# Converting the weights of an attention-and-SoLU kernel two pieces at a time, with a longer search for the order

## The chip, the cores and the metric

The kernel runs on one core of one Trainium2 chip. The time is what the device takes for one execution, in microseconds (us), as a median over runs. A core has engines that run side by side, each through its own instructions in a fixed order: PE multiplies matrices (PEld is its loading of the stationary operand), DVE works on vectors, ACT does activations, scalings and copies, POOL does elementwise work and masks, and SP issues most of the transfers from memory (DMA). An engine waits for another only through semaphores.

## The reference

Attention within a narrow window plus attention to summaries of blocks, then a feed-forward layer whose activation is `h * softmax(h)`, normalised:

```python
k_sum = k.reshape(B, H, nb, block, D).max(axis=3)      # block = 32
v_sum = v.reshape(B, H, nb, block, D).mean(axis=3)
scores = concat([where(|i-j| < 16, scale * q @ k.T, -1e9),
                 scale * q @ k_sum.T + log(32)])
x = softmax(scores) @ concat([v, v_sum])               # 4 x 8 heads x 768 x 64
h = x @ w_in                                           # 3072 x 512 @ 512 x 1024
solu = h * softmax(h)
ln = (solu - mean) / sqrt(var + 1e-6) * g_ln
out = ln @ w_out                                       # 1024 x 512
```

`w_in`, `w_out` and `g_ln` arrive as they are; `w_in` and `w_out` reach the kernel as 64-bit words (the weights are doubles), everything else as 32-bit floats.

## The kernel before

**Tiling.** The 3072 rows are 24 tiles `t` of 128 rows. For each tile two pairs of heads are scored (`scores`, PE tile `s`), exponentiated on ACT, turned (`values_turn`, tile `t`) and multiplied with the values (`values`, tile `x`). The result is split into a high and a low part, `xh` and `xl`, so that three matmuls give one product of nearly full precision. `first(t)` multiplies them with `w_in` into two halves `h` of 512 columns (24 matmuls, L697), takes the maximum, the exponential, the product and the mean (`he`), and gets the reciprocal deviation; `turn(t)` transposes `he` into `lh` and `ll`; `second(t)` multiplies these with `w_out` into `o` (24 matmuls, L775), scales and stores it. `second` runs four tiles behind `first` (LAG).

**Weights.** Each weight matrix is loaded in eight pieces of 128 rows by 512 doubles (`load_w`, L356, on the SP queue), that is 128 x 1024 words. A piece of `w_in` is a row block `c` and a half `nh` of the columns; a piece of `w_out` is a row block `f`. `rounded` (L359) makes a float of each double: the high words are converted on ACT or DVE (L368, L370), the low words likewise (L374, L376), the sign is combined in (L379, DVE), the high part is shifted (L383, DVE) and the two are added (`tt`, L288 on DVE or L289 on POOL). Then `split_w_in` copies the rounded part (`copy`, ACT or DVE) and subtracts it (L288 or L289), and `split_w_out` does the same with the row's `g_ln` as a factor (L400 on ACT, L402 on DVE). The scratch `st` of a piece of `w_in` lies in the five buffers of `he`, that of `w_out` in the two buffers of `vrow`. The result `hl` takes the place of the raw words.

**Order.** The code first collects operations: an engine or several that could do it, a planned cost on each, and what it depends on. `Plan.issue` then simulates the engines with these costs (`order`): at each step the operation that can begin first goes next, ties and some exceptions by a due time `due`, which comes from the operations that need the result; that of an SP load is its place in the program, at the start the string LOADS (`w` a piece of `w_in`, `k` keys, `q` queries, `r` rows of `v` for the means, `v` the first values, `Q` and `V` the next ones). It makes 64 such plans, each with other random noise on all due times, the SP loads' too, and takes the one in which PE ends first. The instructions are issued in that order, and every engine keeps to it. Where the plan has PE idle before 80 us, matmuls of zeros are put in (`keep_up`, L900).

## Time and profile before

| | us |
|---|---|
| median of 3 runs | 397.38 (397.09 to 397.52) |
| profiled execution, its time | 397.45 |
| its span, first to last instruction | 395.7 |
| PE busy | 386.6 (98%) |
| DVE busy | 275.4 (70%) |
| ACT busy | 248.7 (63%) |
| POOL busy | 97.9 (25%) |

The page divides the span in 40 slices of 9.9 us; each digit is the busy share of a slice in tenths:

```profile
PE   8999998999999999999999999999999999999996
DVE  4999998999789866577767657657657654554330
ACT  3889686999798756658558466468466463533411
POOL 4224010416837221236220121221021021101100
DMA  7999992136277320463330410430310000000011
```

PE's row counts matmuls of zeros as busy. DVE and ACT are near full in the first ten slices and at some two thirds or less behind them; the transfers fill the first six. Weights are converted only in those first ten slices.

### The profile page before, as it was taken

Reading aid. Unit: us, or ns where it says so; the run is one execution under the profiler, and the core shown is the slowest. Engines: PE = TensorE matmul, PEld = TensorE weight load, DVE = VectorE, ACT = ScalarE, POOL = GpSimd, SP = SyncE. Lnnn points to the kernel's source line nnn. Section 1 sums busy time; section 2 is a strip of 40 time slices with the busy share of each in tenths; the row PEclk is TensorE's granted clock in tenths of the full one; section 3 lists DMA queues with packets and bytes.
Section 4 is the critical chain, followed back from the end, with each engine's and each line's share of the span. In section 5 each row is a group of like instructions: output and inputs, shape, how many; then the busy total and the mean of one; then the engine's idle time right before and its main releaser. Section 6 shows DMA issues by size and latency. Waiting matters only on the chain.

```text
span 395.7 us, 9677 instructions
## 1 busy us (share of the span) xinstructions
PE 386.6 (98%) x3697; PEld 298.3 (75%) x3703; DVE 275.4 (70%) x884; ACT 248.7 (63%) x746; POOL 97.9 (25%) x245
## 2 busy tenths in 40 slices
PE   8999998999999999999999999999999999999996
PEld 3436766677878888878888888878888887878776
DVE  4999998999789866577767657657657654554330
ACT  3889686999798756658558466468466463533411
POOL 4224010416837221236220121221021021101100
PEclk9999999999999999999999999999999999999999
DMA  7999992136277320463330410430310000000011
GB/s 287 411 410 369 409 329 78 56 113 185 70 248 208 113 103 0 141 175 104 123 112 2 150 66 27 156 73 28 108 48 27 2 28 27 16 12 28 27 55 53
DMA packets 14994, 49.24 MB, mean 124 GB/s; under 512 B 1836, under 2 KB 2092, under 8 KB 13412
## 3 DMA queue, kind: packets, MB, share of 16 engines
q1 hardware_dynamic: 11084, 41.89, 30.8%
q10 hardware_dynamic: 3864, 6.74, 4.7%
q8 instruction: 29, 0.48, 0.5%
q14 instruction: 17, 0.14, 0.1%
HBM read 40.11 MB, written 6.29 MB: 117 GB/s over the span
## 4 chain that ended last, share of the span: by engine, by line
PE 85%; DMA 6%; ACT 3%; DVE 2%; issue 1%; ACTq 1%; SPq 1%; DVEq 0%
PE o L775 35%; PE h L697 30%; PE x L672 6%; PE s L578 5%; PE t L633 3%; PE lt L633 3%; DMA st_v<-in_vr 3%; DMA raw<-in_w_in 2%; DMA vt<-vsum 2%; PE vs_ps L459 1%; PE x L900 1%; ACT he L712 1%; DVE he L720 1%; ACT at L281 1%; PE x L664 1%
## 5 line engine op out<-in xcount | busy, mean ns | idle before, releaser
L775 PE MATMUL o<-w,lh 128*128 128x512 f32 (+1 forms) x400 | 128.0, 390 | 0.1
L697 PE MATMUL h<-w,xh 128*128 128x512 f32 x384 | 127.0, 398 | 0.4 <-DVE he L720 0.4
L605 ACT ACTIVATE e<-e,nm 128x120 f32<-128x120 f32 x192 | 73.1, 385 | 25.0 <-DVE nm L597 25.0
L775 PEld LDWEIGHTS o<-w,lh 128*128 128x128 f32 x400 | 74.1, 188 | 18.5 <-issue 2.4
L697 PEld LDWEIGHTS h<-w,xh 128*128 128x128 f32 x384 | 72.1, 188 | 18.9 <-ACT e L605 0.8
L775 PE MATMUL o<-w,ll 128*128 128x512 f32 (+1 forms) x200 | 76.9, 384 | 0.0
L697 PE MATMUL h<-w,xl 128*128 128x512 f32 x192 | 75.6, 394 | 0.0
L707 DVE TENSOR_REDUCE hm<-h 128x1 f32<-128x512 f32 x48 | 32.6, 686 | 42.7 <-PE h L697 42.7
L281 ACT COPY at<-t 120x512 f32<-120x512 f32 x46 | 24.8, 587 | 46.1 <-PE t L633 45.6
L775 PEld LDWEIGHTS o<-w,ll 128*128 128x128 f32 x200 | 37.6, 188 | 6.6
L697 PEld LDWEIGHTS h<-w,xl 128*128 128x128 f32 x192 | 36.1, 188 | 7.5
L597 DVE CUSTOM_DVE_ANT_0 e<-s,mask 128x120 f32<-128x120 f32 x192 | 40.6, 276 | 1.3 <-PE s L578 1.3
L712 ACT ACTIVATE he<-h,hm 128x512 f32<-128x512 f32 x48 | 32.8, 697 | 9.4 <-DVE hm L709 9.4
L605 ACT ACTIVATION_READ_ACCUMULATOR e<-e,nm 128x1 f32 x192 | 36.5, 190 | 0.0
L760 DVE TENSOR_TENSOR ll<-lt,lh 128x512 fp32r<-128x512 f32 x48 | 31.9, 682 | 6.0 <-ACT lh L281 5.8
L739 POOL TENSOR_SCALAR ss<-ss 128x1 f32<-128x1 f32 x24 | 7.1, 297 | 115.0 <-ACT sq L735 114.9
L720 DVE SCALAR_TENSOR_TENSOR he<-h,hz,he 128x512 f32<-128x512 f32 x48 | 34.1, 746 | 0.4
L672 PE MATMUL x<-at,vt 120*64 120x64 f32 (+1 forms) x768 | 28.3, 225 | 1.5 <-ACT at L281 1.5
L672 PEld LDWEIGHTS x<-at,vt 120*64 120x64 f32 (+1 forms) x768 | 24.6, 138 | 6.3 <-ACT at L281 2.8
L288 DVE TENSOR_TENSOR e<-e,z 128x960 f32<-128x960 f32 x23 | 26.6, 1156 | 0.5
L281 ACT CAST lh<-lt 128x512 fp32r<-128x512 f32 x33 | 18.6, 596 | 12.9 <-PE lt L633 10.0
L735 ACT ACTIVATE sq<-he 128x1024 bf16<-128x1024 f32 x24 | 25.2, 1050 | 0.2
(94 smaller groups left out, 499.6 us busy)
## 6 DMA issues: line engine op xcount, KB each, us to landing
vt<-in_v SPq DMA_DIRECT2D x12, 1024.0 KB, 5.4
kraw<-in_k SPq DMA_DIRECT2D x16, 400.0 KB, 9.1
out<-os ACTq DMA_DIRECT2D x23, 256.0 KB, 2.0
qt<-in_q SPq DMA_DIRECT2D x11, 512.0 KB, 5.5
raw<-in_w_in SPq DMA_DIRECT2D x8, 512.0 KB, 10.7
raw<-in_w_out SPq DMA_DIRECT2D x8, 512.0 KB, 9.5
st_v<-in_vr SPq DMA_DIRECT2D x6, 512.0 KB, 12.5
st_v<-in_vb SPq DMA_DIRECT2D x8, 384.0 KB, 3.3
```

Source lines behind the costliest of these rows:

```text
L281: by = {act: lambda: nc.scalar.copy(out=to(), in_=of()), dve: lambda: nc.vector.tensor_copy(out=to(), in_=of()), pool: lambda: nc.gpsimd.t ...
L288: by = {dve: lambda: nc.vector.tensor_tensor(out=to(), in0=a(), in1=b(), op=kind), pool: lambda: nc.gpsimd.tensor_tensor(out=to(), in0=a() ...
L597: nc.vector.tensor_tensor_reduce(out=e.ap[:, n, :], in0=sc.ap[:, j, (2 * i + up) * KC:(2 * i + up + 1) * KC], in1=mask[:, mi, :], scale=-S ...
L605: nc.scalar.activation(out=e.ap[:, n, :], in_=e.ap[:, n, :], func=AF.Exp, bias=nm.ap[:, n:n + 1], scale=-1.0, accum_out=z.ap[:, n:n + 1])
L672: nc.tensor.matmul(xp()[j * D:(j + 1) * D, i, qs], vs.ap[:k, u, cs], at.ap[:k, u % 2, n[j] + u // 2, :], start=not apart, stop=not apart o ...
L697: nc.tensor.matmul(hp.ap, a.ap[:, c, ts], w.ap[:, i], start=(c == 0 and n == 0), stop=(c == NKC - 1 and n == 2))
L707: op(dve, 0.6, lambda i=i, hp=hp: nc.vector.tensor_reduce(out=nms.ap[:, i:i + 1], in_=hp.ap, op=ALU.max, axis=AX.X, negate=True), r=[hp], ...
L712: op(act, 0.71, lambda i=i, hp=hp: nc.scalar.activation(out=part(i), in_=hp.ap, func=AF.Exp, bias=nm.ap, accum_out=zs.ap[:, i:i + 1]), r=[ ...
L720: op(dve, 0.67, lambda i=i, hp=hp: nc.vector.scalar_tensor_tensor(out=part(i), in0=hp.ap, scalar=zs.ap[:, 0:1], in1=part(i), op0=ALU.mult, ...
L735: op(act, 1.13, lambda: nc.scalar.activation(out=sq.ap, in_=e.ap, func=AF.Square, accum_out=ss.ap), r=[e], w=[sq, ss])
L760: op(dve, 0.6, lambda part=part, r=r: nc.vector.tensor_tensor(out=part(lo), in0=tp.ap[:, r], in1=part(hi).bitcast(F32), op=ALU.subtract), ...
L775: nc.tensor.matmul(o.ap[:, cols], a.ap[:, f, :], w.ap[:, i, cols], start=(f == 0 and n == 0), stop=(f == NFC - 1 and n == 2))
```

## The change

Two neighbouring pieces of a weight matrix share one buffer of raw words, `[P, 2, 1024]`, and one `hl`, `[P, 2, 2, 512]`; they are still loaded by two transfers, but each step of `rounded` is one instruction over the 1024 columns of both. The high and the low words have a buffer of their own each (`st` and `lw`, from the same ring as before). The copy and the subtraction of `w_in` are one instruction for both pieces, the multiplications with `g_ln` stay one for each piece, since the factor differs. `first` and `second` read their piece through `weights(key)`. The planned costs are those of the longer instructions. `w_out` is still converted at the tiles 0 to 3, one pair at each.

The search makes 600 plans. The first has no noise, the next 15 have noise of 10 (before: 3) on all due times, and every further one starts from the noise of the best so far and adds noise to about 2% of the operations. The best is the one with the least sum of PE's end and half the mean end of PE's operations; one that is as good replaces it. LOADS has another order within its first twelve loads.

```diff
-LOADS = "wwkwqkkkqwwwrrrwwvQV"
+LOADS = "wwkqkkqwwkwwrrrwwvQV"
...
-    TRIES, NOISE = 64, 3.0
+    TRIES, NOISE = 600, 10.0
+    FIRST, FEW = 16, 0.02
...
-        due, best = [o.due for o in self.ops], None
-        for seed in range(self.TRIES):
-            noise = random.Random(seed)
-            for o, x in zip(self.ops, due):
-                o.due = x + (noise.gauss(0.0, self.NOISE) if seed else 0.0)
+        due, best, rnd = [o.due for o in self.ops], None, random.Random(0)
+        for i in range(self.TRIES):
+            noise = [x + (rnd.gauss(0.0, self.NOISE) if i < self.FIRST or rnd.random() < self.FEW else 0.0) * (i > 0)
+                     for x in (best[3] if i >= self.FIRST else [0.0] * len(due))]
+            for o, x, n in zip(self.ops, due, noise):
+                o.due = x + n
             order = self.order()
             if order:
-                end = max(o.end for o in order if "pe" in o.can)
-                if best is None or end < best[0]:
-                    best = end, order, [(o.start, o.end, o.engine, o.cost, o.fn) for o in self.ops]
-        _, order, kept = best
+                ends = [o.end for o in order if "pe" in o.can]
+                end = max(ends) + 0.5 * sum(ends) / len(ends)
+                if best is None or end <= best[0]:
+                    best = end, order, [(o.start, o.end, o.engine, o.cost, o.fn) for o in self.ops], noise
+        _, order, kept, _ = best
...
-    COPY_W = ((act, 0.52), (dve, 0.34))
+    COPY_W = ((act, 0.89), (dve, 0.61))
...
-    LO_W = ((dve, 0.6), (pool, 1.4))
-    ADD_W = ((dve, 0.62), (pool, 1.46))
+    LO_W = ((dve, 1.14), (pool, 2.7))
+    ADD_W = ((dve, 1.22), (pool, 2.8))
...
     def load_w(key, src, after=()):
-        raw[key] = x = plan.buf(const, [P, 1024], I32, f"w{key}", 1, f"raw{key}")
-        op(sp, 0.43, lambda: nc.sync.dma_start(out=x.ap, in_=src.bitcast(I32)), w=[x], nbytes=P * 4096,
+        c, i = divmod(key, 2)
+        if i == 0:
+            raw[c] = plan.buf(const, [P, 2, 1024], I32, f"w{c}", 1, f"raw{c}")
+        x = raw[c]
+        op(sp, 0.43, lambda: nc.sync.dma_start(out=x.ap[:, i], in_=src.bitcast(I32)), w=[(x, i)], nbytes=P * 4096,
            after=after)
-    def rounded(key, tag, bufs):
-        x = raw.pop(key)
-        st = plan.buf(sb, [P, 2, 512], I32, tag, bufs, f"cv{key}")
-        words = lambda i: x.ap.rearrange("p (n t) -> p n t", t=2)[:, :, i]
-        high, low = (lambda: st.ap[:, 0]), (lambda: st.ap[:, 1])
-        op(act, 0.57, lambda: nc.scalar.activation(
+    def rounded(c, tag, bufs):
+        x = raw.pop(c)
+        st = plan.buf(sb, [P, 1024], I32, tag, bufs, f"cv{c}")
+        lw = plan.buf(sb, [P, 1024], I32, tag, bufs, f"cl{c}")
+        words = lambda i: x.ap.rearrange("p i (n t) -> p (i n) t", t=2)[:, :, i]
+        high, low = (lambda: st.ap), (lambda: lw.ap)
+        op(act, 0.94, lambda: nc.scalar.activation(
             out=high().bitcast(F32), in_=words(1).bitcast(F32), func=AF.Copy, scale=2.0 ** -112),
-            r=[x], w=[(st, 0)], alt=[(dve, 0.34, lambda: nc.vector.tensor_scalar(
+            r=[x], w=[st], alt=[(dve, 0.61, lambda: nc.vector.tensor_scalar(
                 out=high().bitcast(F32), in0=words(1).bitcast(F32), scalar1=2.0 ** -112, scalar2=None,
                 op0=ALU.mult))], port=True)
-        op(act, 0.57, lambda: nc.scalar.activation(
-            out=low(), in_=words(0).bitcast(U32), func=AF.Copy, scale=2.0 ** -29), r=[x], w=[(st, 1)],
-            alt=[(dve, 0.34, lambda: nc.vector.tensor_scalar(
+        op(act, 0.94, lambda: nc.scalar.activation(
+            out=low(), in_=words(0).bitcast(U32), func=AF.Copy, scale=2.0 ** -29), r=[x], w=[lw],
+            alt=[(dve, 0.61, lambda: nc.vector.tensor_scalar(
                 out=low(), in0=words(0).bitcast(U32), scalar1=2.0 ** -29, scalar2=None, op0=ALU.mult))], port=True)
-        op(dve, 0.6, lambda: nc.vector.scalar_tensor_tensor(
+        op(dve, 1.14, lambda: nc.vector.scalar_tensor_tensor(
             out=low(), in0=high(), scalar=-2 ** 31, in1=low(), op0=ALU.bitwise_and, op1=ALU.bitwise_or),
-            r=[(st, 0)], w=[(st, 1)], port=True)
-        op(dve, 0.34, lambda: nc.vector.tensor_scalar(
+            r=[st], w=[lw], port=True)
+        op(dve, 0.61, lambda: nc.vector.tensor_scalar(
             out=high(), in0=high(), scalar1=3, scalar2=None, op0=ALU.logical_shift_left),
-            w=[(st, 0)], port=True)
-        tt(ADD_W, ALU.add, high, high, low, r=[(st, 1)], w=[(st, 0)], port=True)
-        wt[key] = hl = plan.buf(const, [P, 2, 512], F32R, f"w{key}", 1, f"w{key}")
-        return (lambda: high().bitcast(F32)), st, hl
-    def split_w_in(c, nh):
-        w, st, hl = rounded(c * 2 + nh, "he", NHE)
-        copy(COPY_W, lambda: hl.ap[:, 0], w, r=[(st, 0)], w=[(hl, 0)], port=True)
-        tt(LO_W, ALU.subtract, lambda: hl.ap[:, 1], w, lambda: hl.ap[:, 0].bitcast(F32),
-           r=[(st, 0), (hl, 0)], w=[(hl, 1)], port=True)
+            w=[st], port=True)
+        tt(ADD_W, ALU.add, high, high, low, r=[lw], w=[st], port=True)
+        hl = plan.buf(const, [P, 2, 2, 512], F32R, f"w{c}", 1, f"w{c}")
+        for i in range(2):
+            wt[2 * c + i] = hl, i
+        return (lambda: high().bitcast(F32).rearrange("p (i n) -> p i n", i=2)), st, hl
+    def weights(key):
+        hl, i = wt[key]
+        return (lambda k: hl.ap[:, i, k]), [(hl, (i, 0)), (hl, (i, 1))]
+    def split_w_in(c):
+        w, st, hl = rounded(c, "he", NHE)
+        copy(COPY_W, lambda: hl.ap[:, :, 0], w, r=[st], w=[(hl, (0, 0)), (hl, (1, 0))], port=True)
+        tt(LO_W, ALU.subtract, lambda: hl.ap[:, :, 1], w, lambda: hl.ap[:, :, 0].bitcast(F32),
+           r=[st, (hl, (0, 0)), (hl, (1, 0))], w=[(hl, (0, 1)), (hl, (1, 1))], port=True)
     def split_w_out(f):
-        w, st, hl = rounded(2 * NKC + f, "vrow", 2)
-        gs = g_sb[:, f:f + 1]
-        op(act, 0.61, lambda: nc.scalar.activation(out=hl.ap[:, 0], in_=w(), func=AF.Copy, scale=gs),
-           r=[(st, 0), g_b], w=[(hl, 0)])
-        op(dve, 0.66, lambda: nc.vector.scalar_tensor_tensor(
-            out=hl.ap[:, 1], in0=w(), scalar=gs, in1=hl.ap[:, 0].bitcast(F32),
-            op0=ALU.mult, op1=ALU.subtract), r=[(st, 0), (hl, 0), g_b], w=[(hl, 1)], port=True)
+        w, st, hl = rounded(NKC + f // 2, "vrow", 2)
+        for i in range(2):
+            gs = g_sb[:, f + i:f + i + 1]
+            op(act, 0.61, lambda i=i, gs=gs: nc.scalar.activation(out=hl.ap[:, i, 0], in_=w()[:, i], func=AF.Copy, scale=gs),
+               r=[st, g_b], w=[(hl, (i, 0))])
+            op(dve, 0.66, lambda i=i, gs=gs: nc.vector.scalar_tensor_tensor(
+                out=hl.ap[:, i, 1], in0=w()[:, i], scalar=gs, in1=hl.ap[:, i, 0].bitcast(F32),
+                op0=ALU.mult, op1=ALU.subtract), r=[st, (hl, (i, 0)), g_b], w=[(hl, (i, 1))], port=True)
...
-            w, hp = wt[c * 2 + nh], hs[nh]
+            hp, (w, ws) = hs[nh], weights(c * 2 + nh)
...
-    for i in range(2 * NKC):
-        split_w_in(*divmod(i, 2))
-        if i % 2 == 0 and i < 2 * NPP:
-            run(values_turn(0, 0, i // 2))
-            run(values(0, 0, i // 2, 0, True))
+    for c in range(NKC):
+        split_w_in(c)
+        if c < NPP:
+            run(values_turn(0, 0, c))
+            run(values(0, 0, c, 0, True))
...
-        for f in range(WPT * t, min(WPT * t + WPT, NFC)):
+        for f in range(WPT * t, min(WPT * t + WPT, NFC), 2):
             split_w_out(f)
```

More of the change, by code (lines that the diff above doesn't have):

```diff
@@ L772, in second, with mm @@
             for f in range(NFC):
-                def mm(f=f, w=wt[2 * NKC + f], o=o, cols=cols):
+                w, ws = weights(2 * NKC + f)
+                def mm(f=f, w=w, o=o, cols=cols):
                     for n, (a, i) in enumerate(((hi, 1), (lo, 0), (hi, 0))):
                         nc.tensor.matmul(
-                            o.ap[:, cols], a.ap[:, f, :], w.ap[:, i, cols], start=(f == 0 and n == 0),
+                            o.ap[:, cols], a.ap[:, f, :], w(i)[:, cols], start=(f == 0 and n == 0),
                             stop=(f == NFC - 1 and n == 2))
-                op(pe, 0.69 * k, mm, r=[hi, lo, wt[2 * NKC + f]], w=[o])
+                op(pe, 0.69 * k, mm, r=[hi, lo] + ws, w=[o])
             os = plan.buf(sb, [P, DM], F32, "os", 2, f"os{t}")
```

4 lines of the change are left out of this document (2 added, 2 removed).

## The prediction

> **What bounds the kernel now.** I read the busy time by stage first, then the same table for the filler matmuls alone, then the chain of waits in order of time. The columns of the first two are stretch, length, then busy time and number of instructions of PE, PEld, DVE, ACT and POOL (the second has PE and PEld alone), clock, DMA share, GB/s.
>
> ```profile
> span 395.7 us, 9677 instructions
> ```
> ```profile
> 0.00:10.00 10.00, 8.55 (x57) 3.60 (x58) 4.45 (x8) 3.75 (x5) 4.21 (x18) 1.00 0.79 288
> 10.00:38.30 28.30, 26.36 (x326) 13.29 (x330) 28.13 (x104) 24.75 (x83) 9.01 (x16) 1.00 1.03 401
> 38.30:60.00 21.70, 21.70 (x210) 15.72 (x207) 21.00 (x58) 16.85 (x52) 1.64 (x2) 1.00 1.02 363
> 60.00:97.00 37.00, 34.47 (x386) 25.16 (x386) 35.02 (x115) 32.95 (x89) 12.63 (x28) 1.00 0.33 101
> 97.00:395.70 298.70, 295.56 (x2726) 240.50 (x2724) 186.78 (x603) 170.40 (x520) 70.37 (x181) 1.00 0.24 78
> ```
> ```profile
> 0.00:10.00 10.00, 7.52 (x23) 2.73 (x24) 1.00 0.79 288
> 10.00:38.30 28.30, 10.50 (x44) 4.28 (x48) 1.00 1.03 401
> ...
> 60.00:97.00 37.00, 2.67 (x10) 0.91 (x11) 1.00 0.33 101
> ```
>
> From 97 us on PE stands still for 298.70 - 295.56 = 3.14 us in all, while DVE and ACT have much to spare: nothing in the change shortens that stretch. The loss is ahead of it. Before 38.3 us PE idles 1.45 + 1.94 = 3.39 us and spends 7.52 + 10.50 = 18.02 us on matmuls of zeros (L900). Between 60 and 97 us it idles 2.53 us and spends 2.67 us on zeros. That is 26.6 us in which PE does no work, and meanwhile DVE is full: 28.13 of 28.30 us, then 21.00 of 21.70, then 35.02 of 37.00. So the start is bound by DVE and by the order of its work, the rest by PE. The first `h` matmul ends the first loss:
>
> ```profile
> 26.80 3.55 PE vs_ps L459 x8
> ...
> 38.39 5.79 PE h L697 x24
> ```
> ```profile
> 14.16 0.33 SPq L447 DMA_DIRECT2D st_v<-in_vr  x1
> ```
> ```profile
> st_v<-in_vr SPq DMA_DIRECT2D x6, 512.0 KB, 12.5
> ```
> ```profile
> 34.48 0.58 ACT L281 CAST xh<-x 128x512 fp32r<-128x512 f32 x1
> ...
> 35.20 0.68 DVE L678 TENSOR_TENSOR xl<-x,xh 128x512 fp32r<-128x512 f32 x1
> ...
> 35.94 0.65 PE L664 MATMUL x<-at,vsum 24*64 24x256 f32 x4
> ...
> 38.64 0.69 DVE L288 TENSOR_TENSOR w<-cv,w 128x512 fp32r<-128x512 f32 x1
> ```
>
> Two strands end there together. One is the data: the third `st_v` leaves at 14.16 and lands 12.5 us later, at 26.7; the means follow at 26.80, then the first values, whose bank is free for the second values only after `xl` at 35.2 to 35.9. The other is the weights: the last of `w_in` is split at 38.64. The change touches both, the second directly.
>
> **The change part by part.** Instructions that go: of 16 pieces, each with two conversions, a combine (L379), a shift (L383) and an add, pairs leave half; the copy and the subtraction of `w_in` halve too, L400 and L402 stay at 8 each. What one doubled instruction saves:
>
> ```profile
> L379 DVE SCALAR_TENSOR_TENSOR cv<-cv 128x512 int32<-128x512 int32 x16 | 12.3, 776 | 1.0 <-ACT cv L374 0.6 <-ACT cv L368 0.3
> L288 DVE CUSTOM_DVE_ANT_0 cv<-cv 128x1024 uint16<-128x1024 uint16 x13 | 8.6, 677 | 0.0
> ...
> L288 DVE TENSOR_TENSOR e<-e,z 128x960 f32<-128x960 f32 x6 | 6.9, 1152 | 0.0
> L383 DVE TENSOR_SCALAR cv<-cv 128x512 int32<-128x512 int32 x16 | 6.9, 446 | 0.1
> ...
> L402 DVE SCALAR_TENSOR_TENSOR w<-cv,g_sb,w 128x512 fp32r<-128x512 f32 x8 | 5.8, 745 | 1.1 <-ACT w L400 1.1
> ...
> L288 DVE TENSOR_TENSOR w<-cv,w 128x512 fp32r<-128x512 f32 x7 | 5.0, 718 | 0.8 <-ACT w L281 0.7
> ```
> ```profile
> L368 ACT ACTIVATE cv<-raw 128x512 f32<-128x512 f32 x13 | 8.6, 673 | 3.5 <-DMA raw<-in_w_in 3.0 <-DVE nm L597 0.4
> ...
> L374 ACT ACTIVATE cv<-raw 128x512 int32<-128x512 uint32 x9 | 6.1, 674 | 1.4 <-DMA raw<-in_w_in 1.4
> ...
> L281 ACT CAST w<-cv 128x512 fp32r<-128x512 f32 x7 | 4.3, 608 | 4.1 <-DVE cv L288 4.1
> ...
> L735 ACT ACTIVATE sq<-he 128x1024 bf16<-128x1024 f32 x3 | 3.2, 1063 | 0.0
> ```
> ```profile
> 30.07 0.68 DVE L379 SCALAR_TENSOR_TENSOR cv<-cv 128x512 int32<-128x512 int32 x1
> 30.67 0.68 DVE L288 TENSOR_TENSOR w<-cv,w 128x512 fp32r<-128x512 f32 x1
> ```
> ```profile
> 27.98 0.68 ACT L368 ACTIVATE cv<-raw 128x512 f32<-128x512 f32 x1 [0.34 <-DMA raw<-in_w_in]
> 28.57 0.66 ACT L374 ACTIVATE cv<-raw 128x512 int32<-128x512 uint32 x1
> ```
>
> DVE: two pieces follow each other after 0.60 us and end after 0.60 + 0.68 = 1.28. One over 1024 columns, by the slope from 512 columns (0.68) to the 960 of `e` (1.152), takes 1.22. That saves 0.06 each. Gone from DVE are 8 + 8 + 6.5 + 3.5 (L379, L383, half of 13 adds, half of 7 subtractions) and half of the 32 - 13 - 9 = 10 conversions that ACT does not do: 31, so **1.9 us**. ACT: two end after 0.59 + 0.66 = 1.25, one of 1024 takes about 1.06 (L735), 0.2 saved; half of 22 conversions and 7 copies is 14.5, so 2.9 us. I cost ACT's part at nothing: it has 3.6 us idle between 10 and 38.3 and 4.0 between 60 and 97, and only what the plan then moves over from DVE counts; that lies within the bounds of the search below. Perfetto Trace Analysis of the Trainium skill (Optimizing Scalar/DVE Operations) puts the access cost of an instruction at about 60 ns on DVE and 93 ns on ScalarE; by it the DVE saving would be 1.9 us as well and ACT's an estimated 1.3. The same section says that where these engines leave bubbles elsewhere, breaking instructions up may finish work sooner, which speaks against this change; the rival of late pairs below is that case, and the full DVE speaks for grouping.
>
> Each pair waits for two loads. The SP queue keeps its 16 weight loads, in other places among the others:
>
> ```profile
> 0.79 0.38 SPq L356 DMA_DIRECT2D raw<-in_w_in  x1
> ...
> 3.16 1.69 SPq L356 DMA_DIRECT2D raw<-in_w_in  x3
> ```
> ```profile
> raw<-in_w_in SPq DMA_DIRECT2D x8, 512.0 KB, 10.7
> ```
>
> Before, the first piece left alone, ahead of two `k` and two `q`. A second 0.52 MB at the 288 GB/s of the first stretch is 1.8 us. DVE is idle 5.55 of the first 10 us and has `ksum` to do meanwhile, so the first conversion's lateness costs 0 to 1.8 us of DVE; I take 0.9, the middle, since neither end has a nearer row. Behind the waiting conversion on ACT stand `kw` copies and exponentials, for which DVE waits. Instructions net: 1.9 - 0.9 = **-1.0 us**. Moved queue entries also shift `r`, `v` and `q`; all that is in the search's term.
>
> The search: 64 independent orders become 600, most of them small steps from the best. No row shows its gain, so it is bounded by the losses that an order can remove.
>
> ```profile
> L597 DVE CUSTOM_DVE_ANT_0 e<-s,mask 128x120 f32<-128x120 f32 x32 | 6.7, 272 | 0.0
> ```
>
> Before 38.3 us DVE reduces four pairs of scores (32 instructions, 6.7 us); two belong to the first `h`, so 3.3 us could wait, and the third `st_v` could land earlier. So 0 to -3.3 there. Between 60 and 97 us most of the idle 2.53 us was not in the plan (up to its 80 us a planned gap gets zeros): 0 to -2.5. Upward: an order fitted more closely to planned durations may meet as much unplanned idle again, +2.5. I take about two fifths of the 5.8, **-2.1**: the two strands ended together, so both must improve.
>
> Sum: 397.45 (the profiled execution: span 395.7 and 1.75 around it; the median is 397.38) - 1.0 - 2.1 = **394.3 us**.
>
> **Edits that I cost at nothing.** The `he` ring holds five buffers: a piece took one, a pair takes two, so two and a half pairs of `w_in` can be in flight where five pieces could. Cover: each stretch of DVE holds more ready work than time (28.13 of 28.30), so a pair is seldom wanted sooner; if that cover is gone, the price is a wait of one add, 1.22 us, on DVE. A pair holds both column halves of its rows, so the first half of `h` needs the last pair whole, where before its second piece was wanted 2.8 us later (half of the 5.79 us of the first `h`). Before, the last subtraction began at 38.64 and ended at 39.33, and `h` came to its fourth row block only some 2.1 us after 38.39, at 40.5: 1.2 us of cover, and the pair is ready earlier by the 1.0 us above. If it is gone, the first `h` waits by what is missing, at most the 2.8. The new goal of the search, the end plus half the mean end of PE's work, can trade 1 us at the end for 2 us in the middle; with 295.56 us of PE work behind 97 us that nothing interrupts for long, the two move together, so: nothing.
>
> **The rivals.** (a) *Both losses go*: -1.0, all of -3.3, and 1.9 of the 2.53: 391.2 us. For it: DVE's work may be reordered widely. Against: the work put off is due soon.
> (b) *Hidden*: the plan improves on paper only, and 0.9 of the 1.0 is eaten by late pairs: 397.3 us; the same comes out if more tries find no better order than the 64 did. For it: the unplanned idle.
> (c) *Late pairs of `w_out`, slower*:
>
> ```profile
> L402 DVE SCALAR_TENSOR_TENSOR w<-cv,g_sb,w x8: 734/745/752, 50.5 to 93.0; 128x512 fp32r<-128x512 f32 x8
> ```
> ```profile
> 96.19 0.97 PE o L775 x3
> ```
>
> `vrow` has two buffers: two pieces were in flight, now one pair fills both, and the next pair's high words wait for the last L402 of this one. Eight pieces in 42.5 us is 6.1 each, so a piece spent some 12.1 us in flight, of which its own steps are about 4.0 (0.67 + 0.68 + 0.45 + 0.68 + 0.75 + 0.75, with L400 on ACT taken as long as L402): 8.1 us of waiting. A pair's steps are about 6.3 (1.06 + 1.22 + 0.8 + 1.22 + 1.25 + 0.75); with the same waiting 14.4 per pair against 12.1 per two pieces: 2.3 late each, 6.9 over the three pairs behind the first. The last `o` step follows the end of the last L402 by 2.4 us, so 4.5 reach PE, and half of it is filled with `h`: 397.45 + 2.3 = **399.7 us**. It decides from 12.9 us of residence on (12.1 + a third of 2.4). Against it: the plan knows the buffers and can bring these steps forward.
> (d) *The port*: a POOL add blocks DVE.
>
> ```profile
> 20.05 1.71 POOL L289 TENSOR_TENSOR cv<-cv 128x512 int32<-128x512 int32 x1
> ```
> ```profile
> 20.57 1.75 DVE L379 SCALAR_TENSOR_TENSOR cv<-cv 128x512 int32<-128x512 int32 x1
> ```
>
> Beside it L379 took 1.75 instead of 0.68. A pair's add is twice as long; two of them, each holding DVE for 1.4 us more, take back 2.8: 397.1 us. SBUF — State Buffer of the Trainium skill (Who interferes with whom) says this pair of ports is held for the whole instruction, which these two rows bear out.
>
> **How the numbers follow.** Forecast 0.54 (own range 392.3 to 396.5); (a) 0.16; (b) 0.11; (c) 0.16; (d) 0.03. The range runs from 390.4, a little below (a), to 398.2, over (b) and (d): (c) and the tails, under 0.2, are left out. What a measurement of this kernel tells from no change is about 0.2%, 0.8 us. Faster: 0.54 + 0.16 = 0.70; same: 0.11 + 0.03 = 0.14; slower: 0.16.
>
> **What would show it.** Conversions over 1024 columns at about 1.06 us on ACT and 1.22 on DVE; the first `h` at about 36 us instead of 38.39; L900 and idle before 97 us down by some 3 from 26.6; from the first `o` on nothing changed. Wrong if `h` starts no earlier, if the `o` matmuls stand behind a late L402, or if unplanned idle between 60 and 97 us exceeds 2.53.

## The result, and the profile after

| | before | after |
|---|---|---|
| median of 6 runs each, us | 397.24 (396.67 to 397.52) | 401.05 (400.34 to 402.46) |
| ratio after to before, 95% interval | | 1.0101 [1.0083, 1.0119] |
| profiled execution, us | 397.45 | 401.1 |
| its span, us | 395.7 | 399.3 |

The kernel became slower by 3.8 us. The forecast was 394.3, its range 390.4 to 398.2: wrong in sign, and 2.9 us outside the range. Two single runs of kernels further on, one of 472.36 us at a clock of 0.754 and one of 404.23 at 0.987, stand far above the others of their kernel and are left out of its median and ratio.

Busy time by stage of the kernel after, with the same columns as before; PE is the first pair, DVE the third, ACT the fourth:

```profile
0.00:10.00 10.00, 8.71 (x29) 3.35 (x29) 2.28 (x4) 3.26 (x3) 3.98 (x18) 1.00 0.78 277
10.00:38.30 28.30, 26.15 (x315) 14.07 (x320) 27.31 (x74) 21.60 (x63) 6.66 (x13) 1.00 1.03 398
38.30:60.00 21.70, 20.46 (x242) 13.90 (x243) 19.93 (x63) 20.69 (x63) 8.37 (x10) 1.00 0.94 344
60.00:97.00 37.00, 35.06 (x387) 26.81 (x389) 35.55 (x112) 29.85 (x87) 14.53 (x24) 1.00 0.38 116
97.00:399.30 302.30, 297.71 (x2724) 239.43 (x2722) 180.03 (x589) 182.23 (x533) 65.07 (x181) 1.00 0.23 78
```

The same table for the matmuls of zeros alone (L919 in the new numbering):

```profile
0.00:10.00 10.00, 8.40 (x27) 3.16 (x27) 1.00 0.78 277
10.00:38.30 28.30, 7.69 (x31) 2.94 (x35) 1.00 1.03 398
38.30:60.00 21.70, 2.58 (x8) 0.83 (x11) 1.00 0.94 344
60.00:97.00 37.00, 1.17 (x3) 0.31 (x4) 1.00 0.38 116
```

Ahead of 97 us PE idles 1.29 + 2.15 + 1.24 + 1.94 = 6.62 us and spends 19.84 on zeros: 26.5 us lost, where it was 26.6. Behind 97 us it idles 302.30 - 297.71 = 4.59, 1.45 more than before, and is busy 297.71 for 2724 instructions, where 295.56 did for 2726: 2.15 more. 1.45 + 2.15 is the 3.6 us by which the span grew. So there are two questions: why the start gained nothing, and why the part behind it, which the forecast took for fixed, grew.

**The start.** PE's timeline, after (start, length, instruction, count, and in brackets the idle time ahead of it with what ended it):

```profile
32.47 0.58 PE L714 MATMUL h<-w,xh 128*128 128x512 f32 x1
...
43.79 0.39 PE L714 MATMUL h<-w,xh 128*128 128x512 f32 x1
...
47.63 1.47 PE L919 MATMUL t<-zero 128*128 128x512 bf16 x5
...
51.54 0.62 PE L714 MATMUL h<-w,xh 128*128 128x512 f32 x2
...
60.91 0.50 PE L714 MATMUL h<-w,xh 128*128 128x512 f32 x1 [1.55 <-DVE he L737]
```

and before:

```profile
38.32 0.50 PE L697 MATMUL h<-w,xh 128*128 128x512 f32 x1
...
43.79 0.39 PE L697 MATMUL h<-w,xh 128*128 128x512 f32 x1
...
51.47 0.40 PE L697 MATMUL h<-w,xh 128*128 128x512 f32 x1
```

The first `h` begins 5.85 us earlier, more than forecast. But by the program's order the row at 43.79 is the last matmul of the first tile in both kernels, and the 48th matmul of `h`, the last of the second tile, begins at 51.54 (the first of the two in that row), before at 51.47: nothing of the lead is left. The first `h` ran ahead with the first two pairs of weights alone, which its first twelve matmuls use, and the time won went into zeros such as those at 47.63. Then PE stood for `he` (60.91). What stood ahead of `he` shows in DVE's timeline, after:

```profile
57.17 0.20 DVE L732 TENSOR_SCALAR hz<-hz 128x1 f32<-128x1 f32 x1
57.30 1.97 DVE L287 COPY kw<-kraw 128x768 f32<-128x768 f32 x1
59.19 0.15 DVE L735 RECIPROCAL hz<-hz 128x1 f32<-128x1 f32 x1
59.26 0.93 DVE L456 TENSOR_REDUCE ksum<-kraw 128x24 f32<-128x768 f32 x1
60.11 0.74 DVE L737 SCALAR_TENSOR_TENSOR he<-h,hz,he 128x512 f32<-128x512 f32 x1
```

and POOL's, after:

```profile
56.47 2.37 POOL L294 TENSOR_TENSOR cv<-cv,cl 128x1024 int32<-128x1024 int32 x1
```

The scale of `he` is computed at 57.17, its reciprocal waits behind a `kw` copy of 1.97 us, and `he` behind a further `ksum`. The group of the same copy before:

```profile
L282 DVE COPY kw<-kraw 128x768 f32<-128x768 f32 x2 | 1.1, 528 | 0.0
```

So 1.44 us of the copy go with the POOL add of a pair beside it, which ends 0.4 us ahead of the copy: rival (d) of the prediction, at a place where PE waits. SBUF — State Buffer of the Trainium skill (Who interferes with whom) describes this as a lock on a shared pair of ports; these two rows agree with it.

**DVE's waits ahead of 38.3 us**, after (who waited for what: us in total, times, longest):

```profile
DVE cv L379 <- DMA raw<-in_w_in: 5.1, 1, 5.1
DVE cl L388 <- ACT cl L383: 2.6, 2, 1.7
```

and before:

```profile
DVE cv L376 <- DMA raw<-in_w_in: 3.6, 1, 3.6
```

The first conversion waits 1.5 us longer, and twice a combine waits for a whole pair's conversion on ACT. In these 38.3 us DVE is idle 7.72 + 0.99 = 8.71 us, before 5.55 + 0.17 = 5.72. The instructions of the pairs, after:

```profile
L388 DVE SCALAR_TENSOR_TENSOR cl<-cv,cl 128x1024 int32<-128x1024 int32 x8 | 9.8, 1223 | 2.9 <-ACT cl L383 2.6 <-ACT cv L377 0.2
L383 ACT ACTIVATE cl<-raw 128x1024 int32<-128x1024 uint32 x7 | 8.0, 1142 | 0.0
```

DVE's 1.22 is as forecast, ACT's 1.14 is a little above the 1.06.

**Behind 97 us.** Some 3.1 us of the idle time are the tail behind the last matmul, in both kernels. Ahead of it PE idled 0.06 us before (295.54 busy of 295.60) and 1.53 after (297.67 of 299.20), most of it in one wait (who waited for what: us in total, times, longest):

```profile
PE vs_ps L533 <- DVE ll L777: 1.1, 1, 1.1
```

The extra 2.15 us of busy time lies in the matmuls of `h` and `o`. The clock was 0.999 in both executions. From the start of one matmul to the start of the next, in blocks that nothing interrupts, it is 227 to 230 ns in about half of the blocks before and 231 to 233.5 in the other half; after, nearly all have 231 to 233.5. One block of each kind, before, from the chain of waits (start, length, instruction, count):

```profile
215.08 5.60 PE h L697 x24
...
229.52 5.49 PE h L697 x24
```

The blocks alternate with the two buffers of `lh`, `ll`, `xh` and `xl`, the stationary operands of these matmuls, and buffers get their addresses in the order in which the program first uses them, which the search decides. Their byte addresses modulo 512, two buffers each:

```
            lh         ll         xh         xl
before   160 352    352  96    160  32    160  32
after    160 160    160  96    160  32    160  64
```

The moving operands, the weights, lie at 96 in both. (96 and 352 are the same modulo 256 too, so these numbers do not tell 512 from 256.) So a third suspect, of which the prediction had not thought, stood beside the search and the pairs: where the buffers lie.

### The profile page after: what moved, and what is told of

Its sections match the earlier page's. It is cut to its first block, busy times and chain, and to the rows that moved or that the text cites. A ratio compares the mean times of both kernels' runs of the same rounds, so it can differ in the third digit from the quotient of the medians.

```text
span 399.3 us, 9612 instructions
## 1 busy us (share of the span) xinstructions
PE 388.1 (97%) x3689; PEld 297.6 (75%) x3697; DVE 265.1 (66%) x838; ACT 257.6 (65%) x744; POOL 98.6 (25%) x245
## 5 line engine op out<-in xcount | busy, mean ns | idle before, releaser
L714 PE MATMUL h<-w,xh 128*128 128x512 f32 x384 | 130.7, 401 | 2.1 <-DVE he L737 2.1
L794 PE MATMUL o<-w,lh 128*128 128x512 f32 (+1 forms) x400 | 131.1, 391 | 0.1
L756 POOL TENSOR_SCALAR ss<-ss 128x1 f32<-128x1 f32 x24 | 6.0, 252 | 126.7 <-ACT sq L752 126.6
L286 ACT COPY at<-t 120x512 f32<-120x512 f32 x44 | 23.8, 587 | 19.4 <-PE t L650 18.1
L799 ACT ACTIVATE os<-o,y 128x512 f32<-128x512 f32 (+1 forms) x23 | 15.4, 669 | 22.6 <-PE o L794 17.6
L286 ACT CAST lh<-lt 128x512 fp32r<-128x512 f32 x39 | 21.7, 596 | 10.3 <-PE o L794 7.1
L689 PE MATMUL x<-at,vt 120*64 120x64 f32 (+1 forms) x768 | 28.3, 225 | 0.0
L749 ACT ACTIVATE he<-he,nmu 128x512 f32<-128x512 f32 x22 | 15.6, 723 | 17.5 <-DVE nmu L740 17.5
```

The source lines that it names most:

```text
L286: by = {act: lambda: nc.scalar.copy(out=to(), in_=of()), dve: lambda: nc.vector.tensor_copy(out=to(), in_=of()), pool: lambda: nc.gpsimd.t ...
L689: nc.tensor.matmul(xp()[j * D:(j + 1) * D, i, qs], vs.ap[:k, u, cs], at.ap[:k, u % 2, n[j] + u // 2, :], start=not apart, stop=not apart o ...
L714: nc.tensor.matmul(hp.ap, a.ap[:, c, ts], w(i), start=(c == 0 and n == 0), stop=(c == NKC - 1 and n == 2))
L749: (act, 0.57, lambda sl=sl: nc.scalar.activation(out=e.ap[:, sl], in_=e.ap[:, sl], func=AF.Identity, bias=nmu.ap))], port=True)
L794: nc.tensor.matmul(o.ap[:, cols], a.ap[:, f, :], w(i)[:, cols], start=(f == 0 and n == 0), stop=(f == NFC - 1 and n == 2))
L799: op(act, 0.1 + 0.46 * k, lambda o=o, os=os, cols=cols: nc.scalar.activation(out=os.ap[:, cols], in_=o.ap[:, cols], func=AF.Copy, scale=y.ap),
```

## The experiments

Each was timed in five or more runs (5 to 12) beside the kernel before on the same chip (397.1 to 397.2 us).

**1. The addresses.** A list of names fixes the order in which buffers get their addresses; nothing else changes.

```diff
+PLACE = (
+    "w0_0 w1_0 w2_0 w3_0 w4_0 w5_0 w6_0 w7_0 sel_0 kraw_0 qt_0 kraw_1 he_0 qt_1 lh_0 ksum_0 "
...
+    "hz_3 s1_3 nmu_2 nmu_3 ss_2 y_2 os_1 vacc_0 ss_3 y_3 y_4 vacc_1 y_5 y_6 ")
...
+        self.slots.setdefault(slot, b)
...
+    for x in PLACE.split():
+        plan.slots[x].ap
     plan.idle = idle
```

First both kernels with the addresses exchanged:

> The changed kernel, instruction for instruction, with its buffers put at the addresses that they had before the change (the first use of each buffer decides its address, and the new order moved them). Theory P (place): the addresses of the stationary tiles set the pace of the matmuls behind 97 us; before, the o matmuls of odd tiles followed each other at 227.6 to 228.8 ns and those of even ones at 231.5 to 233.5, h at 229 to 230 in every second pair of tiles, while after nearly all stand at 231 to 233.5. Then the odd o tiles return to about 228 ns and the time falls by about 2.2 us from 401.05 to about 398.9. Theory O (order): the pace follows from the h and o blocks being cut in pieces by the new order; then the pace stays at 231 to 233.5 and the time at about 401.

> The kernel before, instruction for instruction, with its buffers at the addresses of the changed kernel. Theory P: about 2.2 us slower, 399.4 us, with nearly all o steps at 231 to 233.5 ns, the odd tiles too. Theory O: 397.2 us, unchanged, with odd o tiles at about 228 ns.

| | us | ratio to before |
|---|---|---|
| after, at before's addresses | 400.0 | 1.0078 [1.0063, 1.0094] |
| before, at after's addresses | 398.72 | 1.0045 [1.0032, 1.0058] |

Both move the way that the addresses say, by less than the 2.2 us expected: 1.05 us (401.05 to 400.0, where the intervals of the two ratios still overlap) and 1.5.

Then the kernel before with its eight stationary buffers in a row, 4096 bytes apart, all at 96 modulo 512 or, with 256 columns of padding instead of 224, all at 160:

```diff
+    "sel_0 PAD lh_0 lh_1 ll_0 ll_1 xh_0 xh_1 xl_0 xl_1 kraw_0 qt_0 kraw_1 he_0 qt_1 ksum_0 vt_0 "
...
+        if x == "PAD":
+            sb.tile([P, 224], BF16, name="pad", tag="pad", bufs=1)
```

> The kernel before, instruction for instruction; only the addresses differ: the eight buffers from which PE loads its stationary operand (lh, ll, xh, xl, two of each) stand in a row, each at 96 bytes past a multiple of 512. In the traces so far the pace went with that remainder: lh at 352 with ll at 96 gave 227.6 ns, xh and xl at 32 gave 229 to 230, and wherever lh or xh stood at 160 it was 231.5 to 233.5. Theory M (the remainder decides): all o tiles at 227 to 229 ns and h at 228 to 230, some 1.5 us less on the 12 even o tiles and 1.2 us on the 12 slow h tiles: about 394.5 us. Theory N (the place matters through something else, the remainder is chance): a mix of paces as before, 397 us within 1.

> As place96, with the eight buffers 64 bytes further on, at 160 past a multiple of 512. Theory M: all o and h tiles at 231.5 to 233.5 ns, 399 us. Theory N: as place96, 397 us within 1.

| | us | ratio to before |
|---|---|---|
| all at 96 | 394.14 | 0.9927 [0.9907, 0.9946] |
| all at 160 | 399.07 | 1.0052 [1.0033, 1.0071] |

The same instructions in the same order differ by 4.9 us. Behind 97 us, at 96:

```profile
97.00:400.00 303.00, 292.24 (x2726) 240.33 (x2724) 186.42 (x603) 170.30 (x520) 70.39 (x181) 1.00 0.23 77
```

and at 160:

```profile
97.00:400.00 303.00, 297.10 (x2723) 239.90 (x2721) 186.24 (x601) 169.78 (x516) 70.38 (x181) 1.00 0.23 77
```

PE is busy 4.86 us less at 96, and that is the whole difference. A block of 24 matmuls of `h` from the chain of waits, at 96:

```profile
199.49 5.44 PE h L706 x24
```

and at 160:

```profile
200.51 5.60 PE h L706 x24
```

5.44 / 24 is 227 ns for a matmul of `h`, 5.60 / 24 is 233; the block of `o` just ahead took 5.66 us at 96 and 5.80 at 160. The other 64 bytes of padding also move every buffer that lies behind these eight, but of PE's work only the matmuls of `h` and `o` change pace; a `x`, `t` or `s` matmul takes 225, 225 and 269 ns in both runs. So the address of the stationary operand sets the pace, by some 6 ns in 230. Whether it does so alone or by its distance from the moving operand, which lies at 96 in all of these runs, was not tried. The change had moved these buffers as a side effect: put back, it gains 1.05 us, and behind 97 us PE is busy 295.86 again.

**2. The new search and the pairs apart.** All at before's addresses. Pairs with the old search and the new LOADS; single pieces with the new search and the old LOADS:

Against the changed kernel, the first one (with the loop of before):

```diff
-    TRIES, NOISE = 600, 10.0
-    FIRST, FEW = 16, 0.02
+    TRIES, NOISE = 64, 3.0
```

and against the kernel before, the second (with the loop of the change):

```diff
-    TRIES, NOISE = 64, 3.0
+    TRIES, NOISE = 600, 10.0
+    FIRST, FEW = 16, 0.02
```

> Weights in pairs and the new LOADS, but the old search of 64 plans, buffers at the old addresses. Theory S (the new search spoils the order, the pairs gain the 1.0 us of the prediction): about 396.2 us. Theory G (pairs cost: later first conversion, one pair of w_out in flight): 399 to 400 us, with more filler and idle time of PE ahead of 100 us than the 26.6 us before.

> Single pieces and the old LOADS as before, but the new search of 600 plans, buffers at the old addresses. Theory S (the search spoils the order): 398.5 us or more, from idle PE time behind 97 us. Theory G (pairs cost, the search gains its 2.1 us): about 395 us, with 2 us less filler and idle time of PE ahead of 97 us than the 26.6 before.

| | us | ratio to before |
|---|---|---|
| pairs, old search, new LOADS | 403.88 | 1.0168 [1.0141, 1.0194] |
| single pieces, new search, old LOADS | 399.68 | 1.0068 [1.0056, 1.0081] |
| both (the change, same addresses) | 400.0 | 1.0078 [1.0063, 1.0094] |

Each part costs by itself: pairs 6.7 us, well above the 2 to 3 expected, the search 2.5. Together they cost 2.8: the new search takes 3.9 us off the pairs, and on top of the new search pairs cost only 0.3 (400.0 against 399.68, the intervals overlap). So the 2.8 cannot be put down to one of the two. The new search on single pieces shows the loss of the change without any pair: ahead of 97 us PE spends 19.31 us on zeros and idles 7.53, 26.8 as before, and behind it the row is

```profile
97.00:399.00 302.00, 296.76 (x2726) 240.03 (x2724) 182.03 (x590) 179.90 (x533) 69.57 (x184) 1.00 0.24 78
```

that is 5.24 us idle where it was 3.14, and 1.2 more busy. The plans that the two searches chose, in the kernel's own account of costs, end at 395.0 us for the kernel before, 393.3 for the change, 397.5 for pairs with the old search and 392.7 for single pieces with the new one: on paper both results of the new search are better than before, on the chip both are worse.

The new search puts noise on all operations, those of the steady part too, where nothing was to be gained. So the noise was kept to the operations ahead of the seventh tile (`RAMP`, 472, is a place in the list of operations):

```diff
-            noise = [x + (rnd.gauss(0.0, self.NOISE) if i < self.FIRST or rnd.random() < self.FEW else 0.0) * (i > 0)
-                     for x in (best[3] if i >= self.FIRST else [0.0] * len(due))]
+            noise = [x + (rnd.gauss(0.0, self.NOISE) if i < self.FIRST or rnd.random() < self.FEW else 0.0) * (i > 0 and o.prio < self.RAMP)
+                     for o, x in zip(self.ops, best[3] if i >= self.FIRST else [0.0] * len(due))]
```

> The changed kernel at the old addresses (as both_oldplace, 400.0 us), but the search puts noise only on operations ahead of the seventh tile of rows, so the order of the stretch behind some 105 us follows the due times without noise. Theory S (noise on the steady stretch cost it idle time and broken blocks): PE's idle time between 97 us and the tail falls from 1.8 us to under 0.3 and the time to about 398. Theory T (what is lost comes from the start, where the chip does not keep to the plan): about 400, with the loss ahead of 97 us as large as in both_oldplace or larger.

> As ramponly_both, with single pieces and the old LOADS (against single_newsearch_oldloads, 399.7 us). Theory S: idle time of PE between 97 us and the tail falls from 2.1 to under 0.3 us, the time to 397.5 or less; 395.5 if the start gains on the chip what the search sees there. Theory T: 399 to 400.

| | us | ratio to before |
|---|---|---|
| pairs, noise ahead of the seventh tile | 398.69 | 1.0045 [1.0030, 1.0060] |
| single pieces, likewise | 402.26 | 1.0111 [1.0071, 1.0151] |

With pairs, 1.3 us of the 2.8 go. Behind 97 us PE idles 299.60 - 296.43 = 3.17 us in that run, as before the change; with noise everywhere it was 300.80 - 295.86 = 4.94. The start is another one too, since other noise falls on it: 0.57 us more of busy time is left behind 97 us, so the gain is less than the 1.77 of idle time. With single pieces the result is worse, and its runs have two peaks: 398.45 and 399.18 us at a clock of 0.999 and more, 401.96 to 403.72 at 0.996 and less. The profiled run is of the second kind. Its busy time in slices of 5 us:

```profile
125.00:130.00 5.00, 1.34 (x40) 1.20 (x39) 3.43 (x8) 1.10 (x3) 1.59 (x4) 0.86 0.22 76
130.00:135.00 5.00, 5.00 (x40) 3.92 (x34) 4.03 (x22) 4.39 (x9) 3.40 (x6) 0.50 0.00 0
135.00:140.00 5.00, 5.00 (x23) 4.07 (x22) 2.40 (x4) 2.85 (x17) 2.22 (x8) 0.96 0.00 0
```

PE stands 3.66 of 5 us, its longest wait 3.7 us for `at` on ACT; the chain of waits leads back to a load of keys that landed 10.03 us after its issue at 116.41. The granted clock of these slices is 0.86, 0.50 and 0.96. In slices of 1 us it is 0.50 from about 128.6 to 135.4 us and 1.00 around them. Half of these 6.8 us is lost, 3.4, of which some 0.5 falls in the wait itself, which ends at 129.5. So an order that waits once for a late load pays twice. The fast peak, without such a phase, is no slower than the 399.68 of noise everywhere.

**3. No search at all.** One plan without noise (`TRIES = 1`), the old LOADS, stationary buffers at 96: no pairs, pairs in all weights, in `w_in` alone, in `w_out` alone (the matrix without pairs keeps the functions of before). The edit shown is that of the run without pairs; the others set `TRIES` to 1 in the changed kernel.

```diff
-    TRIES, NOISE = 64, 3.0
+    TRIES, NOISE = 1, 3.0
```

> Single pieces, old LOADS, and no search at all: the one order that follows from the due times without noise. The eight stationary buffers stand at 96 past a multiple of 512, as in place96 (394.1 us), here and in the next three, so that the pace of the matmuls is the same in all four. It is the base of the four: without the search some 1 to 3 us more than place96, 395 to 397 us.

> As plain_single, with all weights in pairs. Theory I (pairs of w_in delay the first h: both pieces must have landed and each step is as long as two): 2 to 4 us more than plain_single, lost ahead of 60 us. Theory W (rival c: one pair of w_out in flight): 2 us or more, lost between 60 and 100 us. Theory of the prediction (fewer instructions free 1.0 us): 1 us less than plain_single.

> As plain_single, with only the pieces of w_in in pairs. Theory I: 2 to 4 us more than plain_single, like plain_pairs. Theory W: no more than plain_single, within 0.8.

> As plain_single, with only the pieces of w_out in pairs. Theory I: as plain_single, within 0.8. Theory W: 2 us or more above plain_single, with o matmuls that wait for L419 between 75 and 100 us.

| | us | ratio to before |
|---|---|---|
| none | 397.15 | 0.9998 [0.9982, 1.0015] |
| `w_out` in pairs | 397.93 | 1.0031 [1.0015, 1.0047] |
| `w_in` in pairs | 402.16 | 1.0121 [1.0103, 1.0139] |
| all in pairs | 405.55 | 1.0200 [1.0173, 1.0227] |

The cost is that of `w_in`, 5.0 us, where 2 to 4 were expected; pairs of `w_out` alone cost 0.8, and the two together 8.4, more than their sum. Part of these numbers is clock again. Slices of 5 us of the run with `w_in` in pairs:

```profile
85.00:90.00 5.00, 5.00 (x16) 3.96 (x15) 5.00 (x10) 2.53 (x5) 2.89 (x6) 0.66 0.25 61
...
100.00:105.00 5.00, 4.45 (x25) 3.03 (x26) 4.96 (x13) 4.43 (x19) 4.25 (x6) 0.72 0.09 13
105.00:110.00 5.00, 5.00 (x22) 4.05 (x22) 4.87 (x9) 4.50 (x9) 3.20 (x4) 0.94 0.63 200
```

They stand behind waits of 2.3 us for `he` on DVE and 1.9 for `he` on ACT, and lose 5 x (0.34 + 0.28 + 0.06) = 3.4 us. The profiled run without pairs has 0.80 and 0.86 in two such slices, 1.7 us. So a part of the 5.0 us is clock: the runs whose mean clock was 0.996 took 401.11 and 401.39 with `w_in` in pairs and 397.04 to 398.76 without. The two waits of this run are not waits on the longer steps: ahead of both `he`, at 78 to 84 us and at 94 to 100, DVE's timeline has steps of single pieces of `w_out` and no pair's. Pairs of `w_in` cost time there through the order of what follows them, and these runs do not show how. With all weights in pairs PE's longest wait is for `he` as well, and there a pair's steps do stand ahead of it:

```profile
PE h L722 <- DVE he L745: 3.4, 1, 3.4
```
```profile
83.24 2.16 DVE L400 TENSOR_SCALAR cv<-cv 128x1024 int32<-128x1024 int32 x1
85.43 1.22 DVE L301 CUSTOM_DVE_ANT_0 cv<-cv,cl 128x2048 uint16<-128x2048 uint16 x1
...
87.49 0.75 DVE L745 SCALAR_TENSOR_TENSOR he<-h,hz,he 128x512 f32<-128x512 f32 x1
```
```profile
82.12 2.73 POOL L302 TENSOR_TENSOR e<-e,z 128x960 f32<-128x960 f32 x1 [4.06 <-DVE hm L734]
```

The shift took 2.16 instead of 0.68 beside the POOL multiplication, which ends at 84.85.

**4. What in the pairs costs.** Under the old search, at before's addresses: the old LOADS, and the new LOADS with conversions of one piece each as it lands, while combine, shift, add, copy and subtraction stay over 1024 columns.

```diff
+        half = lambda y, h: y.ap[:, 512 * h:512 * h + 512]
+        for h in range(2):
+            op(act, 0.57, lambda h=h: nc.scalar.activation(
+                out=half(st, h).bitcast(F32), in_=words(1, h).bitcast(F32), func=AF.Copy, scale=2.0 ** -112),
+                r=[(x, h)], w=[(st, h)], alt=[(dve, 0.34, lambda h=h: nc.vector.tensor_scalar(
...
+            op(act, 0.57, lambda h=h: nc.scalar.activation(
+                out=half(lw, h), in_=words(0, h).bitcast(U32), func=AF.Copy, scale=2.0 ** -29),
+                r=[(x, h)], w=[(lw, h)], alt=[(dve, 0.34, lambda h=h: nc.vector.tensor_scalar(
...
```

> Pairs with the old string LOADS and the old search of 64 plans, buffers at the addresses of the kernel before; beside the 403.88 us of the same with the new LOADS. Theory W (pairs themselves cost, the loads' order does not matter much): 402.5 to 405.5. Rival L (the new load order is what delays the start): 400.5 or less.

> As the run of 403.88 us (pairs, new LOADS, old search, old addresses), but the conversions of the raw words are again made piece by piece as each load lands, 512 columns each; combine, shift, add, copy and subtraction stay over 1024 columns. Theory D1 (the pair waits for its second load): most of the 6.7 us that pairs cost under the old search comes back: 398.5 to 400.5. Theory D2 (the steps behind, each twice as long and given on only when both pieces are done, cost it): 402.5 to 405. Between 400.5 and 402.5 both have a part.

| | us | ratio to before |
|---|---|---|
| pairs, old search, old LOADS | 405.97 | 1.0220 [1.0198, 1.0241] |
| pairs, old search, new LOADS | 403.88 | 1.0168 [1.0141, 1.0194] |
| the latter, conversions by piece | 403.66 | 1.0169 [1.0134, 1.0203] |

The new LOADS are not the cause: the pairs are 2.1 us slower without them, in runs whose clock was 0.992 to 1.000; without them the price of pairs under the old search is 8.8 us. Nor is the wait for the second load, as far as a run under another order can tell: without it the time is the same within its interval. By the numbers set out for these runs that is theory D2, the doubled steps, by what is left over and not by a wait that shows it. Stages of the pairs with the old LOADS, to be held against the first two rows of the prediction's table:

```profile
0.00:10.00 10.00, 8.47 (x55) 3.63 (x56) 1.92 (x3) 0.95 (x1) 3.96 (x18) 1.00 0.79 242
10.00:38.30 28.30, 25.48 (x297) 12.01 (x295) 24.74 (x72) 21.18 (x60) 5.44 (x14) 1.00 0.99 388
```

of the pairs with the new LOADS:

```profile
0.00:10.00 10.00, 8.40 (x59) 3.78 (x60) 2.41 (x4) 2.94 (x3) 3.99 (x18) 1.00 0.81 279
10.00:38.30 28.30, 26.16 (x320) 12.87 (x320) 25.46 (x74) 20.45 (x64) 9.72 (x16) 1.00 1.02 392
```

and of conversions by piece:

```profile
0.00:10.00 10.00, 8.76 (x33) 3.59 (x33) 4.37 (x7) 3.84 (x5) 3.96 (x18) 1.00 0.78 275
10.00:38.30 28.30, 25.90 (x320) 13.04 (x319) 24.36 (x61) 18.38 (x53) 4.17 (x12) 0.94 1.03 403
```

With pairs and the old LOADS DVE is idle 8.08 us of the first 10 instead of 5.55, and 3.56 of the next 28.3 instead of 0.17; with the new LOADS 7.59 and 2.84. Conversions by piece give back the first (4.37 busy, before 4.45) and not the second (3.94 idle). DVE has run out of ready work. With the old LOADS that hangs on the pairs: two waits for a whole pair on ACT, 2.0 us for a copy and 1.7 for a conversion. In the run by piece it does not: 2.6 of the 3.94 are one wait for the sums of the softmax, and 1.7 us of PE's clock went in this stretch (0.94). Perfetto Trace Analysis of the Trainium skill (Optimizing Scalar/DVE Operations) has both rules, that larger operations help an engine that is saturated and smaller ones an engine that is not but holds up others; in the first 38.3 us these rows put DVE under the second once its work comes in pairs.

**5. The change at the fast addresses**, as it is and with the noise ahead of the seventh tile alone:

> The changed kernel as it is, all instructions and their order kept, but with the eight stationary buffers of PE (lh, ll, xh, xl) in a row at addresses that are 96 modulo 512, as in the fastest run so far. Theory P (address sets pace, the order's losses are apart from it): 1176 matmuls of h and o by some 5 ns each come off 401.05, so 395.2 to 396.8 us, and the kernel still stays 1 to 2.5 us above the 394.14 of the kernel before with the same addresses; that rest is the price of the change itself. Rival N (pace and order interact: the new order was only slow because of its pace): below 394.5.

> Pairs, the new loads and the new search with noise only on the operations ahead of the seventh tile, with the eight stationary buffers at 96 modulo 512. Theory P with the two terms added: 398.69 at the old addresses less the 3.1 that these addresses brought the kernel before gives 395.6 (395.0 to 396.2): slower than 394.14, so that pairs are no gain even with the steady part left as it was. Rival: below 394.0, the best version is with pairs.

| all at 96 | us | ratio to before |
|---|---|---|
| the change | 396.96 | 1.0009 [0.9991, 1.0026] |
| the change, noise ahead of the seventh tile | 395.89 | 0.9975 [0.9963, 0.9986] |
| the kernel before (experiment 1) | 394.14 | 0.9927 [0.9907, 0.9946] |

At equal addresses the change costs 396.96 - 394.14 = 2.8 us, the same as at the old addresses (400.0 - 397.2): pace and order add up. 1.1 of it goes with the noise on the steady part, 1.75 is what is left of the pairs and the start. The expectation for the first run was missed by 0.2 at its upper end. The fastest of all kernels is the old one with its stationary buffers at 96; it beats both.

## Why the prediction was wrong

**What bounds the kernel** was half right. The start is bound by DVE and its order; but "nothing in the change shortens that stretch" was taken to mean that nothing lengthens it, and both new losses of the span lie there: 2.15 us of pace and 1.45 of idle time.

**Instructions, -1.0.** The durations came out (DVE 1.22; ACT 1.14 instead of 1.06, so 0.11 saved where 0.2 was taken, at no consequence). The late first pair cost DVE 1.5 us, not 0.9, within the bounds given. So what was added up here was right and small; what the pairs cost lay in the next term.

**Edits costed at nothing: the first of two steps that failed.** The prediction put the cover in DVE's full stretch (28.13 of 28.30), "so a pair is seldom wanted sooner", with 1.22 us as the price of its loss. That fullness was a property of the work in single pieces. In pairs DVE idles 3.0 us more ahead of 38.3 us in the change, and 5.9 more under the old search and LOADS (8.08 + 3.56 against 5.72); under the new search single pieces leave it idle 6.9 (10 - 4.60 + 28.3 - 26.81), pairs 8.7. The price of pairs, forecast at -1.0 in all, was 6.7 us under the old search, 8.4 without any (5.0 for `w_in` alone), and 0.3 on top of the new search, which orders around them. Also costed at nothing was the search's reach into the steady part, where the prediction weighed the new goal and not the noise: 1.3 us.

**The search, -2.1: the second.** Alone, on single pieces, it lost 2.5 us. That this is the size of its upper bound, +2.5 for "an order fitted more closely to planned durations", is luck: the bound stood for idle time between 60 and 97 us, where this run's zeros and idle time come to 5.7 us after 5.2 before, and its loss lies behind 97. Ahead of 97 us nothing was gained, in the change as in the search alone. The first `h` at 32.47 shows that the forecast start can be had (36 was expected), and the zeros ahead of 38.3 us fell from 18.02 to 16.09. Between 38.3 and 60 us 2.58 us of zeros and 1.24 idle came back, where nothing had been lost before: the first tile ended at 43.79 as before, and then `he` was late, behind a blocked copy. The two strands into the first `h` were treated as the loss itself, and nobody asked what would be late after it.

**The rivals.** (c) was on the right side and near in size (399.7), but that is luck: pairs of `w_out` alone cost 0.8 us, and no `o` is among PE's longer waits in the change. (d) occurred once beside a pair's add, with 1.44 us on DVE ahead of the `he` that PE waited 1.55 us for; it had been priced as eating up a gain, not as a wait of PE. (a) did not come. Of (b) the mechanism came, a plan that improves on paper only (393.3 against 395.0), at a larger price than 397.3.

**Not in the prediction at all:** the addresses, 1.05 us. Nothing in the diff names them; they follow from the order.

So the 3.8 us are: addresses 1.05 (1.5 by the exchange the other way), noise on the steady part 1.1 to 1.3, and some 1.5 to 1.75 that are left. Added up the other way, from the kernel before, they are the search 2.5, pairs on top of it 0.3, and addresses 1.05. Each run with another part has another order, so these terms hold for the orders found. Open is how the 1.5 to 1.75 split between the doubled steps, the late first pair, the blocked copy and the start that the search chose, since every kernel tried gets an order of its own; why pairs of both weights cost more than the sum of each; and what in the chip makes an address fast.

## What to carry to other kernels

Ask of a full engine whether it would stay full if its work came in larger lots; halving the instructions buys their fixed cost (0.06 us each on DVE here) and can cost a multiple of it in waits. A search over orders should have noise only where there is something to gain. And a better end of a plan is not yet a gain: 393.3 and 392.7 on paper, against 395.0, were 400.0 and 399.7 on the chip, against 397.2. Before comparing two orders, fix the buffers' addresses: 4.9 us of 394 lay between two placements of the same instructions, more than everything that the change did.

## What the runs showed of the hardware

The pace of back-to-back matmuls over 512 columns depended on the address of the stationary operand modulo 512: about 227 ns for `h` at 96, 233 at 160, with the same instructions in the same order; in the kernel before, `xh` and `xl` at 32 gave near 229, `lh` at 352 with `ll` at 96 near 228. Other residues, and other places of the moving operand, were not tried.

A wait of PE of 2 to 4 us was often, not always, followed by a phase at half the clock. The values between 0.5 and 1 in the rows above are means over 5 us: in slices of 1 us, from 84 to 90 us of the run with `w_in` in pairs, the clock is 1.00, 0.55, 0.50, 0.50, 0.74 and 1.00, which is 3.4 us at 0.50 and costs 1.7; after the 3.7 us above it was 6.8 us. After a wait of 1.55 us in the change, and of 2.9 in the pairs with the old search and the new LOADS, the clock stayed at 1.00. TensorE: Matmul & The Clock Gate of the Trainium skill (The HAM clock gate) describes a clock that falls to half after an idle window of about 3.4 us; the 0.50 agrees, and the phases above last one and two such windows; but they also followed waits that were shorter, as the 2.3 us above.
